# Widening the weights of an attention-and-feed-forward kernel with one shift-or instead of three bit operations

## The chip, the cores and the metric

The kernel runs on one core of one Trainium2 chip. The metric is device microseconds of one execution, from the program's start to its end as the runtime times it; a profile of one further execution gives, beside its own time, the span from its first to its last instruction. Engines are named as the profile names them: PE (TensorE matmul), PEld (its weight loads), DVE (VectorE), ACT (ScalarE), POOL (GpSimd) and SP (SyncE, which issues every DMA here).

## The reference

Attention with 4 sink keys and a window of 128 keys over 4 batches, 8 heads, 768 positions and head size 64, then a feed-forward layer over the 3072 tokens:

```python
keep = is_sink | in_window                 # first 4 keys, or 0 <= query - key < 128
a = softmax(np.where(keep, q @ k.T / 8, -1e9))
x = (a @ v) laid out as [3072, 512]
h = x @ w_in                               # [512, 2048]
g = np.where(h > 0, h, np.exp(np.minimum(h, 0)) - 1)
out = g @ w_out                            # [2048, 512]
```

The two weight matrices arrive as float64. They are 2 x 8 MB, and reach the kernel as 32 pieces of 128 rows by 512 doubles, viewed as int64.

## The kernel before, in words

**Stages.** The 24 token tiles of 128 are cut into 9 chunks of 2, 2, 2, 3, 3, 3, 3, 3, 3 tiles (`SIZES`, L42). For each chunk `attention(c)` (L503) produces x, and `feed_forward` (L756) runs over 16 steps f. A step is 12 matmuls with the w_in piece 2f into a bank h (L773), an exponential on ACT (L781), two operations that make the activation g (L783 on DVE or POOL, L784 on DVE), a float16 copy gh (L787, ACT), its float16 remainder gl (L794, POOL), and the matmuls with the w_out piece 2f+1 into banks acc (L801). Chunk 0 runs steps 0 to 6, chunk 1 steps 0 to 12, and then each its rest (`PARTS`, L45), so that chunk 0's first steps take the weight pieces as they come. Everything numeric is split into a float16 and a float16 remainder.

**The weights.** `weights(k)` (L437) makes piece k in these steps. SP loads it (L442) into one of 6 tiles raw, 128 rows of 1024 int32, that is 4 KB a row. `weight_f32` (L301) turns doubles into float32 in a tile wv: ACT reads the upper words as float32 and writes them scaled into a PSUM bank acc (L309); DVE moves 13 bits down out of the low words (L310) and the sign out of the high words (L311) into a tile wu; DVE shifts the ACT result by 3 and ORs wu into it (L312). ACT then makes the float16 part w (L463), and POOL the remainder in two halves (L464). A piece is needed by PE once its halves are there. A load waits until its raw tile is free, and until piece k - 5 has its float16 part (`AHEAD`, L50).

**The checks.** The kernel also tests that the numbers are in range: DVE reduces w (L841), the values v, which SP loads a second time into one of two tiles vm (9 loads at L845, 36 reductions at L846), and the keys and queries of chunks 4 to 8, loaded a second time likewise (20 pairs of loads at L856, 20 reductions at L860). `in_range` (L864) sums it up on DVE (L866 to L872), a matmul over the partitions follows (L882), and `decide` (L874). A branch at the very end takes `general_path` (L946) if a test fails; here it doesn't.

**What sets the order.** Every step is a task of the class `Plan` (L103) with an engine, a cost in us, its dependencies and the rings of buffers that it uses. `Plan.order` (L137) lists the tasks by assumed costs and due times, and `keep_order` (L924) fixes that order on each engine, SP's queue included: each engine runs strictly in this order, and an instruction that waits holds up all behind it. PE tasks have places of their own (`pos`), but the lines of scores, values and steps may pass each other. Where the plan leaves PE idle in the first 100 us, `with_idle_products` (L900) puts small matmuls of a constant tile hot (L886) ahead of the next step. Changed costs or dependencies thus move instructions on all engines.

Of the kernel before, what the change touches and what calls it, by code (L numbers as in the profile page):

```python
# [362 lines left out]
def fast_path(tc, ctx, first, kq, vx, wt, out, low, spread, numbers, flag):  # L363
# [68 lines left out]


    w_done = {}
    first_acc2 = []

    def weights(k):  # L437
        raw, v = raws[slot("raw")], wv[slot("wv")]

        def load():  # L440
            if wide:
                nc.sync.dma_start(raw, wt[k].bitcast(I32))  # L442
            else:
                nc.sync.dma_start(raw[:, :512].bitcast(F32), wt[k])

        def step(i):
            return lambda: weight_f32(nc, v, acc[2], wu[k % RINGS["wu"]], raw)[i]()

        ld = add("SP", 0.4, load, deps=[w_done.get(k - AHEAD, [None])[0]], lat=1.45)
        if wide:  # L450
            a = add("ACT", act_us(512), step(0), deps=[ld])
# [3 lines left out]
            ring("wu", [u1, u2], [b])  # L455
            ring("wps", [a], [b])
            ring("raw", [ld], [a, u1, u2])
            first_acc2.append(b)
# [383 lines left out]
    for c, ch in enumerate(CHUNKS):  # L842
        t, n = vm[slot("vm")], len(ch) * P
        src = vx[:, ch[0] * VT : (ch[-1] + 1) * VT].rearrange("p (g w) -> p g w", g=len(ch))
        ld = add("SP", 0.4, lambda t=t, n=n, src=src: nc.sync.dma_start(t.rearrange("p a w -> p (a w)")[:, : NP * n].rearrange("p (g w) -> p g w", w=VT), src), deps=[exps_done[NF * 4 + 8 * c]], lat=dma_us(P * NP * n * 4))  # L845
        new = [add("DVE", dve_us(n), lambda t=t, n=n, p=p, k=c * NP + p: nc.vector.tensor_reduce(v_top[:, k : k + 1], t.rearrange("p a w -> p (a w)")[:, p * n : (p + 1) * n], AX.X, ALU.max, apply_absolute_value=True), deps=[ld]) for p in range(NP)]  # L846
        ring("vm", [ld], new)
        seen += new
    for i in range((len(SIZES) - DUP) * NP):
        c, p = DUP + i // NP, i % NP  # L850
        t, n = vm[slot("vm")].rearrange("p a w -> p (a w)"), len(key_tiles(CHUNKS[c])) * KW + len(CHUNKS[c]) * P

        def both_heads(t=t, n=n, c=c, p=p):
# [92 lines left out]
def general_path(tc, ctx, kq, vx, wt, out, nw):  # L946

    nc = tc.nc
    WS = 1.0 / 256.0 if wt.dtype != F32 else 1.0
# [31 lines left out]
    wo = const.tile([P, NF, DM], F32, name="g_wo")  # L981
    for k in range(NW):
        f = k // 2
        raw = sb.tile([P, 1024], I32, name=f"g_raw{k}", tag="g_raw")
        if wt.dtype != F32:
            u = sb.tile([P, 512], I32, name=f"g_u{k}", tag="g_u")
            v = sb.tile([P, 512], F32, name=f"g_v32_{k}", tag="g_v32")
            nc.sync.dma_start(raw, wt[k].bitcast(I32))
            for step in weight_f32(nc, v, v, u, raw):
                step()  # L990
        else:
            v = raw[:, :512].bitcast(F32)
            nc.sync.dma_start(v, wt[k])
# [182 lines left out]
```

## Time and profile before

| | |
|---|---|
| time, median of 3 runs | 639.71 us (639.65 to 640.58) |
| the profiled execution's own time | 641.82 us |
| its span | 640.0 us, 13460 instructions |
| granted clock, mean | 0.987 of full speed |
| busy: PE, DVE, ACT, POOL | 615.8, 473.7, 416.6, 289.7 us |
| DMA | 95.06 MB, mean 149 GB/s |

The page gives busy times as shares of the whole span. Stages differ, so they are read below by stretches of the span. "Granted clock" is the share of TensorE's full speed that the chip allowed; 0.5 is its lower level. A busy time of PE contains matmuls at either level, and the constant products too. The DMA share is the mean share of time in which the 16 DMA engines had packets under way.

### The profile page before, as it was taken

To read this page: it belongs to the slowest core of one execution; us is meant where nothing else is said; L and a number is where in the kernel's file an instruction comes from. 1 tells how busy PE (TensorE), PEld (TensorE's weight loads), DVE (VectorE), ACT (ScalarE), POOL (GpSimd) and SP (SyncE) were. 2 spreads that over 40 slices of the span, in tenths; PEclk is the share of its full clock that TensorE was granted. 3 is DMA by queue.
4 is the path that set the end of the run, shared out by engine and by line. 5 is a ranking of instruction groups with operands and counts; after the bars stand their busy time and mean duration, and the time that the engine had idled before them with its cause. 6 is when DMAs were issued, how large, how long until landed. Compare 5 with 4: busy or idle time off the path is not lost. (4 is left out here: it accounts for less than half of the span.)

```text
span 640.0 us, 13460 instructions
## 1 busy us (share of the span) xinstructions
PE 615.8 (96%) x4537; PEld 361.2 (56%) x4537; DVE 473.7 (74%) x1248; ACT 416.6 (65%) x1192; POOL 289.7 (45%) x587
## 2 busy tenths in 40 slices
PE   7978999999999999999999999999999999999993
PEld 5645666666665555555555555555555555555551
DVE  7999899876678866687777967788777877555443
ACT  5888787877678766677667666677667666332320
POOL 4578789764334444344334445343334444222220
PEclk9978999999999999999999999999999999999997
DMA  8598858467457944475536746374425654465431
GB/s 306 154 301 224 234 220 253 135 158 185 93 127 133 198 99 107 90 210 110 117 82 158 180 96 156 82 214 106 129 74 139 162 105 100 109 189 137 115 94 61
DMA packets 120863, 95.06 MB, mean 149 GB/s; under 512 B 98132, under 2 KB 98132, under 8 KB 120788
## 3 DMA queue, kind: packets, MB, share of 16 engines
q1 hardware_dynamic: 120788, 94.14, 57.7%
q8 instruction: 37, 0.61, 0.4%
q14 instruction: 38, 0.31, 0.2%
HBM read 63.18 MB, written 7.34 MB: 110 GB/s over the span
## 5 line engine op out<-in xcount | busy, mean ns | idle before, releaser
L773 PE MATMUL h<-x,w 128*128 128x384 f16 (+1 forms) x1728 | 276.6, 310 | 3.3 <-DVE g L784 1.6
L773 PEld LDWEIGHTS <-w 128*128 128x128 f16 x1728 | 168.1, 98 | 98.1 <-POOL w L464 3.3
L794 POOL TENSOR_TENSOR gl<-g,gh 128x384 f16<-128x384 f32 (+1 forms) x144 | 125.1, 869 | 171.5 <-ACT gh L787 127.8
L801 PE MATMUL acc<-w,gh 128*128 128x512 f16 x768 | 194.2, 382 | 0.8 <-ACT gh L787 0.8
L781 ACT ACTIVATE g<-h 128x384 f32<-128x384 f32 (+1 forms) x144 | 65.3, 453 | 82.5 <-PE h L773 70.2
L787 ACT ACTIVATE gh<-g 128x384 f16<-128x384 f32 (+1 forms) x144 | 69.5, 482 | 74.4 <-DVE g L784 72.5
L801 PEld LDWEIGHTS <-gh 128*128 128x128 f16 x768 | 72.6, 98 | 74.8 <-ACT gh L787 3.7
L801 PE MATMUL acc<-w,gl 128*128 128x512 f16 x384 | 109.9, 381 | 0.2 <-POOL gl L794 0.2
L677 DVE SCALAR_TENSOR_TENSOR pq<-e,st,pq 128x256 f16<-128x256 f32 (+1 forms) x176 | 95.8, 572 | 17.3 <-ACT pq L676 16.9
L626 ACT ACTIVATE e<-e,st 128x264 f32<-128x264 f32 (+1 forms) x192 | 93.2, 486 | 14.5 <-DVE st L624 13.3
L624 DVE CUSTOM_DVE_ANT_0 e<-s,m 128x264 f32<-128x264 f32 (+1 forms) x192 | 71.5, 405 | 33.0 <-PE s L604 25.3
L784 DVE SCALAR_TENSOR_TENSOR g<-g,h 128x384 f32<-128x384 f32 (+1 forms) x144 | 72.7, 505 | 18.1 <-POOL g L783 16.7
L676 ACT ACTIVATE pq<-e,st 128x256 f16<-128x256 f32 (+1 forms) x176 | 77.2, 482 | 4.3 <-DVE st L631 3.5
L783 POOL TENSOR_SCALAR g<-g 128x384 f32<-128x384 f32 (+1 forms) x81 | 44.1, 544 | 71.0 <-ACT g L781 65.7
L801 PEld LDWEIGHTS <-gl 128*128 128x128 f16 x384 | 37.7, 98 | 46.4 <-issue 0.8
L783 DVE TENSOR_SCALAR g<-g 128x384 f32<-128x384 f32 (+1 forms) x63 | 25.1, 399 | 38.3 <-ACT g L781 38.1
L464 POOL TENSOR_TENSOR w<-wv,w 128x256 f16<-128x256 f32 x64 | 48.1, 767 | 5.6 <-ACT w L463 5.2
L532 ACT ACTIVATE kq<-kqs 128x912 f16<-128x912 f32 (+1 forms) x40 | 36.0, 913 | 17.6 <-PE s L604 15.2
L630 POOL TENSOR_SCALAR st<-st 128x2 f32<-128x2 f32 x77 | 20.0, 260 | 58.7 <-ACT e L626 55.8
L860 DVE TENSOR_REDUCE checks<-vm 128x1 f32<-128x912 f32 (+1 forms) x20 | 20.8, 1046 | 26.0 <-DMA vm<-in_kq_dram 26.0
L709 PE MATMUL po<-pt,vh 128*64 128x128 f16 x656 | 36.5, 223 | 2.3 <-DMA pt<-pq 2.3
L626 ACT ACTIVATION_READ_ACCUMULATOR e<-e,st 128x1 f32 x192 | 36.0, 188 | 0.0
(93 smaller groups left out, 658.1 us busy)
## 6 DMA issues: line engine op xcount, KB each, us to landing
raw<-in_wt_dram SPq DMA_DIRECT2D x32, 512.0 KB, 5.2
kqs<-in_kq_dram SPq DMA_DIRECT2D x24, 456.0 KB, 3.7
kqs<-in_kq_dram SPq DMA_DIRECT2D x20, 390.0 KB, 3.7
vs<-in_vx_dram SPq DMA_DIRECT2D x28, 256.0 KB, 3.3
out_dram<-wv SPq DMA_DIRECT2D x24, 256.0 KB, 2.9
vm<-in_kq_dram SPq DMA_DIRECT2D x24, 228.0 KB, 3.7
vm<-in_vx_dram SPq DMA_DIRECT2D x6, 768.0 KB, 5.1
vm<-in_kq_dram SPq DMA_DIRECT2D x16, 195.0 KB, 3.4
```

The costliest lines, as they stand in the source:

```text
L464: tls = [add("POOL", pool_us(256), lambda c=c: nc.gpsimd.tensor_tensor(w[k][:, 1, c], v[:, c], w[k][:, 0, c], ALU.subtract), deps=[th]) fo ...
L624: red = add("DVE", 0.24 + 0.001 * wd, lambda ee=ee, me=me, sp=sps[e], m=m, wd=wd, to_score=to_score: nc.vector.tensor_tensor_reduce(ee, sp ...
L626: ex = add("ACT", 0.47 + 0.00085 * wd, lambda ee=ee, me=me, rs=rs[:, e : e + 1]: nc.scalar.activation(ee, ee, AF.Exp, bias=me, scale=-1.0, ...
L676: a = add("ACT", act_us(nb * P, True), lambda src=src, hi=hi, re=re: nc.scalar.activation(hi, src, AF.Copy, scale=re), deps=[rr])
L677: b = add("DVE", 0.478 if nb == 2 else 0.33, lambda src=src, hi=hi, lo=lo, re=re: nc.vector.scalar_tensor_tensor(lo, src, re, hi, ALU.mult ...
L773: nc.tensor.matmul(hp[:, :n], win[:, part, d, :], xx[:, :n], start=k == 0, stop=k == 3 * ND - 1)
L781: a = add("ACT", act_us(n) + 0.18, lambda gf=gf, hp=hp, sums=sums: nc.scalar.activation(gf, hp[:, :n], AF.Exp, scale=1.0 / G_SCALE, accum_ ...
L783: b = add("DVE", 0.14 + 0.00057 * n, lambda gf=gf: nc.vector.tensor_scalar(gf, gf, -1.0, G_SCALE, ALU.add, ALU.mult), deps=[a], slow=2.1, ...
L784: b = add("DVE", dve_us(n), lambda gf=gf, hp=hp: nc.vector.scalar_tensor_tensor(gf, gf, 0.0, hp[:, :n], ALU.min, ALU.max), deps=[b])
L787: th = add("ACT", act_us(n), lambda gf=gf, gh=gh: nc.scalar.activation(gh[:, :n], gf, AF.Copy), deps=[b])
L794: tls.append(add("POOL", pool_us(cut), lambda gl=gl, gf=gf, gh=gh, cut=cut: nc.gpsimd.tensor_tensor(gl[:, :cut], gf[:, :cut], gh[:, :cut], ...
L801: nc.tensor.matmul(acc[i], gg[:, i * P : (i + 1) * P], wout[:, part, :], start=f == f0 and k == 0, stop=f == f1 - 1 and k == 2)
```

## The change

`weight_f32` becomes two operations. The load puts the 4096 bytes of a row 2 bytes into the tile raw (now 1025 words), so that bits 16 to 47 of each double form an aligned 32-bit word. ACT reads the top 16 bits of each double as a bfloat16 and writes it, doubled, as a float16 pattern into the upper half of each word of wu, whose lower halves were set to zero at the start by two POOL memsets. DVE shifts the aligned words of raw right by 13 and ORs the words of wu into them. L310, L311, and the PSUM bank as a stop on the way, are gone. The factor 256 of the weights is in the pattern now, in the general path 1.

The checks' loads get other dependencies: of the values chunk by chunk after exponentials 64 + 3c instead of 64 + 8c, of keys and queries after 92 + 2i instead of 94 + 2i, counted over the 144 steps in their order; and the plan assumes 2 us more for a load of keys and queries.

```diff
-def weight_f32(nc, v, d, u, raw):
-    ui = u.bitcast(U16).rearrange("p (f t) -> p f t", t=2)
-    words = raw.rearrange("p (f t) -> p f t", t=2)
-    halves = raw.bitcast(U16).rearrange("p (f t) -> p f t", t=4)
+def weight_f32(nc, v, top, raw, scale):
+    shifted = raw.bitcast(U16)
     return (
-        lambda: nc.scalar.activation(d, words[:, :, 1].bitcast(F32), AF.Copy, scale=2.0**-111),
-        lambda: nc.vector.tensor_scalar(ui[:, :, 0], halves[:, :, 1], 13, None, ALU.logical_shift_right),
-        lambda: nc.vector.tensor_scalar(ui[:, :, 1], halves[:, :, 3], 0x8000, None, ALU.bitwise_and),
-        lambda: nc.vector.scalar_tensor_tensor(v.bitcast(I32), d.bitcast(I32), 3, u, ALU.logical_shift_left, ALU.bitwise_or),
+        lambda: nc.scalar.activation(top.bitcast(F16)[:, 1::2], shifted.bitcast(BF16)[:, 4 : 4 * 512 + 1 : 4], AF.Copy, scale=scale),
+        lambda: nc.vector.scalar_tensor_tensor(v.bitcast(U32), raw.bitcast(U32)[:, 1:1025:2], 13, top.bitcast(U32), ALU.logical_shift_right, ALU.bitwise_or),
     )
+def load_weights(nc, raw, piece):
+    if piece.dtype != F32:
+        nc.sync.dma_start(raw.bitcast(U16)[:, 1:2049], piece.bitcast(U16))
...
+    for t in wu:
+        nc.gpsimd.memset(t, 0)
...
-            u1 = add("DVE", 0.446, step(1), deps=[ld], slow=2.0)
-            u2 = add("DVE", 0.446, step(2), deps=[ld], slow=2.0)
-            b = add("DVE", 0.7, step(3), deps=[a, u1, u2])
+            b = add("DVE", 0.13 + 0.00108 * 512, steps[1], deps=[a], slow=1.5)
...
-    evacs[2] = first_acc2[-1] if first_acc2 else None
...
-        ld = add("SP", 0.4, lambda t=t, n=n, src=src: ..., deps=[exps_done[NF * 4 + 8 * c]], lat=dma_us(P * NP * n * 4))
+        check_v(c, exps_done[NF * 4 + 3 * c])
-        ld = add("SP", 0.8, both_heads, deps=[exps_done[len(exps_done) - 50 + 2 * i]], lat=dma_us(P * n * 4))
+        ld = add("SP", 0.8, both_heads, deps=[after], lat=2.0 + dma_us(P * n * 4))
+        check_kq(DUP + i // NP, i % NP, len(SIZES) * NP + i, exps_done[NF * 6 - 4 + 2 * i])
```

Since the plan's costs change, the order changes on every engine. Of the constant products, 62 stand in PE's order before and 29 now. Three places follow. Line numbers of the changed kernel differ by a few: L765, L775, L776 and L793 are the old L773, L783, L784 and L801.

DVE, the last steps of chunk 8, before: L860 reduces a second load of keys and queries, L783 and L784 make the activation g, L866 is the first operation of `in_range`.

```order
L784 SCALAR_TENSOR_TENSOR g_113<-g_113,h_168 128x384
L783 TENSOR_SCALAR g_114<-g_114 128x384
L784 SCALAR_TENSOR_TENSOR g_114<-g_114,h_169 128x384
L860 TENSOR_REDUCE checks<-vm_93 128x1
L783 TENSOR_SCALAR g_113<-g_113 128x384
L784 SCALAR_TENSOR_TENSOR g_113<-g_113,h_168 128x384
L860 TENSOR_REDUCE checks<-vm_93 128x1
L783 TENSOR_SCALAR g_114<-g_114 128x384
L866 TENSOR_SCALAR checks<-checks 128x144
```

The same place with the change, up to the first operation of `in_range` (L862 now):

```order
L776 SCALAR_TENSOR_TENSOR g_114<-g_114,h_169 128x384
L775 TENSOR_SCALAR g_113<-g_113 128x384
L776 SCALAR_TENSOR_TENSOR g_113<-g_113,h_168 128x384
L775 TENSOR_SCALAR g_114<-g_114 128x384
L776 SCALAR_TENSOR_TENSOR g_114<-g_114,h_169 128x384
L775 TENSOR_SCALAR g_113<-g_113 128x384
L776 SCALAR_TENSOR_TENSOR g_113<-g_113,h_168 128x384
L775 TENSOR_SCALAR g_114<-g_114 128x384
L862 TENSOR_SCALAR checks<-checks 128x144
```

The reductions of loads no longer stand between the last steps: the last one is 24 rows ahead of L862, with eleven L776 between them.

SP's queue from its twelfth row on, before: raw are the weight loads, kqs keys and queries, vs values, pt a transpose for the values' matmuls.

```order
L524 DMA kqs_63<-in_kq_dram 128x520
L524 DMA kqs_64<-in_kq_dram 128x520
L442 DMA raw_135<-in_wt_dram 128x1024
L442 DMA raw_130<-in_wt_dram 128x1024
L524 DMA kqs_63<-in_kq_dram 128x652
L524 DMA kqs_64<-in_kq_dram 128x652
L442 DMA raw_131<-in_wt_dram 128x1024
L524 DMA kqs_63<-in_kq_dram 128x652
L546 DMA vs_65<-in_vx_dram 128x512
L695 DMA_TRANSPOSE pt_109<-pq_106 128x9x128
L524 DMA kqs_64<-in_kq_dram 128x652
L442 DMA raw_133<-in_wt_dram 128x1024
```

The same place with the change:

```order
L516 DMA kqs_63<-in_kq_dram 128x520
L516 DMA kqs_64<-in_kq_dram 128x520
L314 DMA raw_135<-in_wt_dram 128x2048
L314 DMA raw_131<-in_wt_dram 128x2048
L314 DMA raw_130<-in_wt_dram 128x2048
L516 DMA kqs_63<-in_kq_dram 128x652
L314 DMA raw_133<-in_wt_dram 128x2048
L516 DMA kqs_64<-in_kq_dram 128x652
L314 DMA raw_132<-in_wt_dram 128x2048
L516 DMA kqs_63<-in_kq_dram 128x652
L314 DMA raw_135<-in_wt_dram 128x2048
L538 DMA vs_65<-in_vx_dram 128x512
```

Of these twelve loads six are weights now, where four were.

POOL's start, before, from the memset of the constant tile ones to the end of the identity matrix:

```order
L407 MEMSET ones 128x128
L408 MEMSET hot 128x256
masks.py:197 MEMSET ident 128x128
L411 MEMSET pq_104 128x128
L411 MEMSET pq_105 128x128
L411 MEMSET pq_106 128x128
masks.py:199 AFFINE_SELECT ident<-ident 128x128
```

The same place with the change:

```order
L410 MEMSET ones 128x128
L412 MEMSET wu_128 128x512
L412 MEMSET wu_129 128x512
L413 MEMSET hot 128x256
masks.py:197 MEMSET ident 128x128
L416 MEMSET pq_104 128x128
L416 MEMSET pq_105 128x128
L416 MEMSET pq_106 128x128
masks.py:199 AFFINE_SELECT ident<-ident 128x128
```

Two memsets of 512 words each stand ahead of the rest.

## Rows read from the trace of the kernel before

**Rows 1.** The span in five stretches: us, busy (x instructions) by engine, clock, DMA.

```profile
0.00:28.00 28.00, 23.32 (x169) 16.19 (x170) 23.18 (x97) 19.06 (x60) 13.47 (x43) 1.00 0.71 240
28.00:70.00 42.00, 34.07 (x291) 21.51 (x289) 38.45 (x98) 34.21 (x99) 33.62 (x64) 0.88 0.93 253
70.00:120.00 50.00, 49.08 (x379) 32.10 (x377) 44.83 (x106) 41.27 (x116) 39.72 (x71) 1.00 0.72 223
120.00:600.00 480.00, 479.11 (x3559) 276.96 (x3558) 351.86 (x915) 314.87 (x902) 196.21 (x403) 1.00 0.56 132
600.00:640.00 40.00, 30.17 (x149) 14.47 (x147) 15.38 (x34) 7.19 (x20) 6.72 (x9) 0.92 0.27 77
```

**Rows 2.** The same columns, PE, PEld and POOL alone: constant products, 28 to 70 us.

```profile
28.00:70.00 42.00, 4.17 (x37) 3.11 (x35) 0.00 (x0) 0.88 0.93 253
```

**Rows 3.** Who PE waited for, 28 to 70 us: total, times, longest.

```profile
PE s L609 <- DVE st L624: 4.3, 2, 3.7
PE h L773 <- DVE g L784: 1.6, 1, 1.6
PE h L773 <- POOL w L464: 1.1, 1, 1.1
```

**Rows 4.** Timeline of PE, 42 to 75 us: start, us, operation, count.

```profile
42.51 2.74 PE L773 MATMUL h<-x,w 128*128 128x256 f16 x12
...
56.35 2.33 PE L773 MATMUL h<-x,w 128*128 128x256 f16 x11 [1.11 <-POOL w L464]
...
73.53 1.47 PE L773 MATMUL h<-x,w 128*128 128x256 f16 x12
```

**Rows 5.** Groups of instructions by line and shape: busy us, mean ns, idle before.

```profile
L312 DVE SCALAR_TENSOR_TENSOR wv<-acc,wu 128x512 int32<-128x512 int32 x32 | 21.8, 681 | 1.3 <-ACT acc L309 1.2
...
L310 DVE TENSOR_SCALAR wu<-raw 128x512 uint16<-128x512 uint16 x32 | 20.3, 634 | 0.2 <-DMA raw<-in_wt_dram 0.2
...
L309 ACT ACTIVATE acc<-raw 128x512 f32<-128x512 f32 x32 | 20.1, 629 | 1.8 <-DVE wv L312 1.6
...
L463 ACT ACTIVATE w<-wv 128x512 f16<-128x512 f32 x32 | 19.8, 619 | 0.3 <-DVE wv L312 0.3
...
L558 DVE SCALAR_TENSOR_TENSOR vl<-vs,vh 128x512 f16<-128x512 f32 x23 | 18.2, 799 | 0.8 <-ACT vh L557 0.7
...
L846 DVE TENSOR_REDUCE checks<-vm 128x1 f32<-128x384 f32 x24 | 12.2, 537 | 0.0
```

**Rows 6.** DVE busy with L310, L311 and L312 alone, by stretch.

```profile
0.00:28.00 28.00, 7.48 (x14) 1.00 0.71 240
28.00:70.00 42.00, 17.46 (x28) 0.88 0.93 253
```

**Rows 7.** Timeline of POOL and DVE at the start.

```profile
1.55 0.30 POOL L408 MEMSET hot<- 128x256 bf16 x1
...
2.39 0.28 POOL masks.py:199 TENSOR_SCALAR_AFFINE_SELECT ident<-ident 128x128 f32<-128x128 f32 x1
```

**Rows 8.** The same, DVE's first instruction.

```profile
1.23 1.53 DVE L331 CAST pt<-pt 128x128 f32<-128x128 int32 x1 [1.23 <-POOL pt L328]
```

**Rows 9.** Timeline of PE, a score matmul of chunk 0's third pair of heads.

```profile
14.75 0.49 PE L609 MATMUL s<-kqs 64*128 64x132 f32 x4 [0.20 <-DMA kqs<-in_kq_dram]
```

**Rows 10.** Timeline of the last steps, ACT, DVE and PE.

```profile
623.04 0.19 ACT L781 ACTIVATION_READ_ACCUMULATOR g<-h 128x1 f32 x1
...
625.47 0.81 PE L801 MATMUL acc<-w,gl 128*128 128x512 f16 x3
625.58 1.10 DVE L860 TENSOR_REDUCE checks<-vm 128x1 f32<-128x912 f32 x1 [3.37 <-DMA vm<-in_kq_dram]
...
626.60 0.35 DVE L783 TENSOR_SCALAR g<-g 128x384 f32<-128x384 f32 x1
...
629.33 0.61 PE L801 MATMUL acc<-w,gh 128*128 128x512 f16 x2 [0.84 <-ACT gh L787]
```

**Rows 11.** DMA issues, 28 to 70 us: count, KB each, median us to landing.

```profile
raw<-in_wt_dram SPq DMA_DIRECT2D x11, 512.0 KB, 4.8
```

More of the change, by code (lines that the diff above doesn't have):

```diff
@@ L14 @@
 U16 = mybir.dt.uint16
+U32 = mybir.dt.uint32
 AF = mybir.ActivationFunctionType
@@ L296, in dma_us @@
     return nbytes / 330e3
-def weight_f32(nc, v, d, u, raw):
-    ui = u.bitcast(U16).rearrange("p (f t) -> p f t", t=2)
-    words = raw.rearrange("p (f t) -> p f t", t=2)
-    halves = raw.bitcast(U16).rearrange("p (f t) -> p f t", t=4)
+def weight_f32(nc, v, top, raw, scale):
+    shifted = raw.bitcast(U16)
     return (
-        lambda: nc.scalar.activation(d, words[:, :, 1].bitcast(F32), AF.Copy, scale=2.0**-111),
-        lambda: nc.vector.tensor_scalar(ui[:, :, 0], halves[:, :, 1], 13, None, ALU.logical_shift_right),
-        lambda: nc.vector.tensor_scalar(ui[:, :, 1], halves[:, :, 3], 0x8000, None, ALU.bitwise_and),
-        lambda: nc.vector.scalar_tensor_tensor(v.bitcast(I32), d.bitcast(I32), 3, u, ALU.logical_shift_left, ALU.bitwise_or),
-    )
+        lambda: nc.scalar.activation(top.bitcast(F16)[:, 1::2], shifted.bitcast(BF16)[:, 4 : 4 * 512 + 1 : 4], AF.Copy, scale=scale),
+        lambda: nc.vector.scalar_tensor_tensor(v.bitcast(U32), raw.bitcast(U32)[:, 1:1025:2], 13, top.bitcast(U32), ALU.logical_shift_right, ALU.bitwise_or),
+    )
+def load_weights(nc, raw, piece):
+    if piece.dtype != F32:
+        nc.sync.dma_start(raw.bitcast(U16)[:, 1:2049], piece.bitcast(U16))
+    else:
+        nc.sync.dma_start(raw[:, :512].bitcast(F32), piece)
 def elu(nc, g, h, scale):
@@ L393, in fast_path @@
     wu = rows("wu", [P, 512], I32)
-    raws = rows("raw", [P, 1024], I32)
+    raws = rows("raw", [P, 1025], I32)
     w = rows("w", [P, 2, 512], F16, NW)
@@ L434, in fast_path @@
     w_done = {}
-    first_acc2 = []
     def weights(k):
         raw, v = raws[slot("raw")], wv[slot("wv")]
[L440 to L449, printed above, removed]
-        if wide:
-            a = add("ACT", act_us(512), step(0), deps=[ld])
-            u1 = add("DVE", 0.446, step(1), deps=[ld], slow=2.0)
-            u2 = add("DVE", 0.446, step(2), deps=[ld], slow=2.0)
-            b = add("DVE", 0.7, step(3), deps=[a, u1, u2])
[L455 to L458, printed above, removed]
+        top = wu[k % RINGS["wu"]]
+        ld = add("SP", 0.4, lambda: load_weights(nc, raw, wt[k]), deps=[w_done.get(k - AHEAD, [None])[0]], lat=1.45)
+        if wide:
+            steps = weight_f32(nc, v, top, raw, 2.0)
+            a = add("ACT", act_us(512), steps[0], deps=[ld])
+            b = add("DVE", 0.13 + 0.00108 * 512, steps[1], deps=[a], slow=1.5)
+            ring("wu", [a], [b])
+            ring("raw", [ld], [a, b])
         else:
@@ L841, in fast_path, with check_v, check_kq, both_heads @@
     seen = [add("DVE", 0.5, lambda k=k: nc.vector.tensor_reduce(w_top[:, k : k + 1], w[k][:, 0, :], AX.X, ALU.max, apply_absolute_value=True), deps=[w_done[k][0], exps_done[NF * 4 + 2 * k]]) for k in range(NW)]
[L842 to L846, printed above, removed]
-        ring("vm", [ld], new)
[L848 to L853, printed above, removed]
+    def check_v(c, after):
+        t, n = vm[slot("vm")].rearrange("p a w -> p (a w)"), SIZES[c] * P
+        src = vx[:, CHUNKS[c][0] * VT : (CHUNKS[c][-1] + 1) * VT].rearrange("p (g w) -> p g w", g=SIZES[c])
+        ld = add("SP", 0.4, lambda: nc.sync.dma_start(t[:, : NP * n].rearrange("p (g w) -> p g w", w=VT), src), deps=[after], lat=dma_us(P * NP * n * 4))
+        new = [add("DVE", dve_us(n), lambda p=p, k=c * NP + p: nc.vector.tensor_reduce(v_top[:, k : k + 1], t[:, p * n : (p + 1) * n], AX.X, ALU.max, apply_absolute_value=True), deps=[ld]) for p in range(NP)]
+        ring("vm", [ld], new)
+        seen.extend(new)
+    def check_kq(c, p, k, after):
+        t, n = vm[slot("vm")].rearrange("p a w -> p (a w)"), len(key_tiles(CHUNKS[c])) * KW + SIZES[c] * P
+        def both_heads():
             for e in range(2):
@@ L856, in both_heads @@
                 nc.sync.dma_start(t[r, :n], kq[r, o : o + n])
-        k = len(SIZES) * NP + i
-        ld = add("SP", 0.8, both_heads, deps=[exps_done[len(exps_done) - 50 + 2 * i]], lat=dma_us(P * n * 4))
-        new = [add("DVE", dve_us(n), lambda t=t, n=n, k=k: nc.vector.tensor_reduce(v_top[:, k : k + 1], t[:, :n], AX.X, ALU.max, apply_absolute_value=True), deps=[ld])]
+        ld = add("SP", 0.8, both_heads, deps=[after], lat=2.0 + dma_us(P * n * 4))
+        new = [add("DVE", dve_us(n), lambda: nc.vector.tensor_reduce(v_top[:, k : k + 1], t[:, :n], AX.X, ALU.max, apply_absolute_value=True), deps=[ld])]
         ring("vm", [ld], new)
-        seen += new
+        seen.extend(new)
+    for c in range(len(SIZES)):
+        check_v(c, exps_done[NF * 4 + 3 * c])
+    for i in range((len(SIZES) - DUP) * NP):
+        check_kq(DUP + i // NP, i % NP, len(SIZES) * NP + i, exps_done[NF * 6 - 4 + 2 * i])
     def in_range():
@@ L948, in general_path @@
     nc = tc.nc
-    WS = 1.0 / 256.0 if wt.dtype != F32 else 1.0
+    WS = 1.0
     const = ctx.enter_context(tc.tile_pool(name="g_const", bufs=1))
@@ L983, in general_path @@
         f = k // 2
-        raw = sb.tile([P, 1024], I32, name=f"g_raw{k}", tag="g_raw")
+        raw = sb.tile([P, 1025], I32, name=f"g_raw{k}", tag="g_raw")
+        load_weights(nc, raw, wt[k])
         if wt.dtype != F32:
@@ L987, in general_path @@
             v = sb.tile([P, 512], F32, name=f"g_v32_{k}", tag="g_v32")
-            nc.sync.dma_start(raw, wt[k].bitcast(I32))
-            for step in weight_f32(nc, v, v, u, raw):
+            nc.gpsimd.memset(u, 0)
+            for step in weight_f32(nc, v, u, raw, 1.0):
                 step()
@@ L992, in general_path @@
             v = raw[:, :512].bitcast(F32)
-            nc.sync.dma_start(v, wt[k])
         dst = wo[:, f, :] if k % 2 else wi[:, :, f * P : (f + 1) * P]
```

## The prediction, made before the changed kernel was run

> **What bounds the kernel now.** The first view to read is the table of stretches, because the page's shares hide where PE is idle. From 120 to 600 us PE is busy 479.11 of 480 us [rows 1]: nothing is to be had there, and whatever other engines save there costs or gives nothing. From 70 to 120 us it idles 0.9 us. The three places with room are the first 28 us (4.7 us idle), 28 to 70 us (7.9 us idle, and the only long stretch where the clock falls, to 0.88), and the last 40 us (9.8 us idle). So the question is what the change does in the first 70 us and in the last 20.
>
> In 28 to 70 us chunk 0's first seven steps take the weight pieces as they come, beside chunk 1's attention. DVE is busy 38.45 of 42 us, ACT 34.21, POOL 33.62, and the DMA share is 0.93 [rows 1]. DVE is the fullest, and the waits of PE agree: 4.3 us for L624, 1.6 us for L784, both on DVE, 1.1 us for POOL's half of a weight piece [rows 3]. There is more loss than those waits. After each of the two long stalls PE runs at the lower level, 1.2 GHz: twelve L773 take 2.74 us where 1.47 is normal at full speed, eleven 2.33 where 1.47 x 11/12 = 1.35 would be [rows 4]. These two groups alone lose 1.27 + 0.98 = 2.25 us. And 4.17 us go to constant products [rows 2], which are no work.
>
> At the end, the order of DVE sets it. The last step's exponential and its sum are done at 623.23, but L783 starts at 626.60, because a reduction of a second load (L860) stands ahead of it and waited 3.37 us for its DMA. PE has finished everything else at 626.28 and starts the last step's L801 at 629.33 [rows 10].
>
> **The change part by part.** The profiled execution spans 640.0 us and took 641.82 us itself; the median is 639.71. I sum against the span, and carry the difference to the median.
>
> *Price of a piece on DVE.* Removed: L310 at 634 ns, and L311, the same operation on other halves. L312 at 681 ns becomes one shift-or of the same 512 columns, both inputs in SBUF now. It is not in the trace. Its nearest row is L558, same width and both inputs in SBUF: 799 ns against 681 for L312, which reads PSUM [rows 5]. Bounds 0.68 to 0.80; I take 0.80, the row with the same kinds of inputs. A piece saves 1.27 - 0.12 = 1.15 us of DVE. On ACT a 512-column copy into PSUM (629 ns, L309) becomes one into SBUF (619 ns, L463) [rows 5]: nothing.
>
> *The start.* Two memsets of 512 words are new on POOL, ahead of the rest of its constants. L408 takes 0.30 us for 256 columns [rows 7], so 0.5 to 0.6 us each, about 1.05 together. Who waits? DVE's first cast takes 1.53 us for 128 columns and ends at 2.76, right after POOL's run of small operations ends at 2.39 + 0.28 = 2.67 [rows 7, 8]; it seems to be held until POOL pauses. All masks and the first scores come behind it. Cost between 0 and +1.05; I take **+1.0**.
>
> *0 to 28 us.* The three operations take 7.48 us of DVE [rows 6], of which four L312 are 2.7; so 4.8 go, and 0.5 come back: 4.3 us less of 23.18. DVE is not last everywhere: the third pair's scores wait for their keys at 14.75 [rows 9], and relief before that is lost. Bounds 0 and -4.3; roughly half the stretch lies behind that wait: **-2**.
>
> *28 to 70 us.* 17.46 us [rows 6], less ten L312 (6.8), are 10.65 us removed; 1.2 come back: 9.5 us less. DVE then has 29.0 us of work, and something else is last. If it is ACT, whose 34.21 us nothing shortens, the stretch can give 7.8 us; if the DMA engines' 0.93 is all work, 2.9; if the wait only changes its name, nothing. I take **-6**: PE's two waits for DVE are 5.9 us [rows 3], and the 2.25 us of lower clock and part of the 4.17 us of constant products (33 of 62 are gone from the order) are room for the new wait. The earlier weight loads in SP's queue help; a late transpose ahead of them holds them up as before.
>
> *The middle.* The value checks come in 24 steps of 144, where they came in 64. Six more loads' reductions fall there, 24 x 0.537 = 12.9 us [rows 5] on about 107 us (24/144 of the span, an estimate). DVE goes from 351.86/480 = 73% [rows 1] to some 85%, less than the 90% of 70 to 120 us beside a gapless PE. Cost 0 to 1 us; I take 0, PE's stock of ready steps hides it.
>
> *The end.* No reduction of a load stands in DVE's last 24 rows before the tests. L783 can start at 623.23 instead of 626.60. From its start to L801 it was 629.33 - 626.60 = 2.73 us, with the tests between; so L801 would be ready at 625.96, and PE is free at 626.28, plus 0.16 for the matmul of the tests. L801 at 626.45: **-2.9**. Below that lies nothing but a late DMA again (0).
>
> Sum: +1.0 - 2 - 6 - 2.9 = -9.9. That is 630.1 us of span, and **629.8 us** for the median.
>
> *A rule against the change.* Before, each weight row lands at the tile's start; now 2 bytes on, and no row of before shows such a landing. The Trainium skill ("Collectives: The Full Stack", Rules for kernel authors) asks for buffers at 32-byte multiples, since otherwise the hardware reads, modifies and writes; that speaks against the shifted load, and no run here shows it yet. The Trainium skill ("DMA: Bandwidth & Descriptors", How a descriptor splits into AXI transactions) counts only one more transaction for a 4096-byte row that starts off a 256-byte boundary, 129 beats for 128, an estimate of under 1%, and by that the sum stays as it is.
>
> **The rivals.**
>
> A. *Another engine is last at once.* ACT, the DMA engines or SP's queue take over in the first 70 us. For it: ACT is at 81%, DMA at 0.93 [rows 1]. Against it: at 70 to 120 us PE runs without gaps beside ACT at 83% and DVE at 90%. Then only start and end count: 639.7 + 1.0 - 2.9 = 637.8 us.
>
> B. *The full relief.* The first stretch gives its 4.3, the second the 7.8 that ACT allows: 639.7 + 1.0 - 4.3 - 7.8 - 2.9 = 625.7 us. Against it: strict orders rarely let an engine run full.
>
> C. *Slower: the shifted load.* If a row landing 2 bytes on costs the DMA engines more, weights come late. At 253 GB/s [rows 1] a 512 KB load takes 2.07 us of all engines; 11 are issued in 28 to 70 us [rows 11], 22.8 us, and the stretch has 0.07 x 42 = 2.9 us to spare. At twice the cost it grows by 19.9 us: 639.7 + 1.0 + 19.9 - 2.9 = 657.7. The gain elsewhere is -1.9 with start and end alone, so this rival decides from 4.8 us more in 11 loads, that is 21% more for each. For it stands no row, only that the landing is new; against it, the rows stay 4096 bytes long, and their number stays.
>
> D. *The change doesn't do what it says:* the shift-or takes 1.95 us, as the three did. Then the early terms vanish, and it is case A.
>
> **How the numbers follow.** My forecast (near 630, its own range 626 to 634) has 0.58. A with D has 0.22, B 0.10, C 0.07, and 0.03 are for no difference. 0.2% (1.3 us, about what a measurement here can tell from none) puts the border of "faster" at 638.4. A at 637.8 lies just inside, so I count a fifth of it as the same. Faster: 0.58 + 0.10 + 0.17 = 0.85; same 0.05 + 0.03 = 0.08; slower 0.07. The range must reach to A and B, since forecast alone leaves more than 2 in 10 out: 624.5 to 638.0, which also takes in the bounds of the start and of the stretch to 70 us.
>
> **What would show it.** Right: L310 and L311 gone and the shift-or at 0.7 to 0.8 us; DVE in 28 to 70 us well below 38; PE without gaps from about 61 us on; no dip of the clock at 40 and 57 us; L801's last group within 0.2 us of the group before it. The cast at the start ends near 3.8 us. Wrong: weight loads that land in over 6 us in that stretch (C); PE idle and clock as before with ACT, POOL or a DMA named as its releaser (A); a DVE that again waits for a DMA in the last ten steps (the end's term).

## The result and the profile after

The changed kernel takes 631.99 us (median of 4 runs, 631.36 to 632.39), the kernel before on the same chip 639.68 us (639.19 to 640.58, 4 runs). The ratio is 0.9868, with a 95% interval of 0.9851 to 0.9885. The forecast was 629.8 us in a range of 624.5 to 638.0. The profiled execution took 632.12 us, and its span is 9.7 us shorter than before. That is more than the 7.7 us between the medians, because the profiled execution of the kernel before took 641.82 us, 2.1 us above its median; differences between the two traces hold this too.

The page of the changed kernel, its span and part 1, and below it the five stretches, with the columns of [rows 1]:

```profile
span 630.3 us, 13327 instructions
PE 608.5 (97%) x4504; PEld 357.1 (57%) x4504; DVE 451.4 (72%) x1187; ACT 418.8 (66%) x1192; POOL 291.2 (46%) x586
```

```profile
0.00:28.00 28.00, 20.38 (x141) 13.90 (x143) 21.50 (x81) 18.80 (x53) 18.30 (x49) 1.00 0.77 263
28.00:70.00 42.00, 36.13 (x315) 22.73 (x316) 31.05 (x96) 34.97 (x103) 30.26 (x68) 0.96 0.90 242
70.00:120.00 50.00, 48.95 (x375) 31.62 (x373) 39.05 (x85) 42.52 (x114) 40.05 (x68) 1.00 0.79 230
120.00:600.00 480.00, 479.69 (x3559) 277.19 (x3558) 351.80 (x903) 316.30 (x909) 197.42 (x399) 1.00 0.56 136
600.00:630.30 30.30, 23.30 (x123) 11.68 (x121) 8.03 (x25) 6.23 (x17) 5.23 (x6) 0.93 0.08 29
```

To compare them, PE's constant products must come off its busy time. The same view of their line alone (PE, PEld, clock, DMA), before in the first and third stretch, and after in the first two (it has none later):

```profile
0.00:28.00 28.00, 4.46 (x27) 2.88 (x27) 1.00 0.71 240
...
70.00:120.00 50.00, 0.34 (x4) 0.07 (x1) 1.00 0.72 223
```

```profile
0.00:28.00 28.00, 4.82 (x25) 2.88 (x25) 1.00 0.77 263
28.00:70.00 42.00, 0.58 (x4) 0.31 (x4) 0.96 0.90 242
```

Idle time and constant products together are the time in which PE has no work of the task: 28 - 23.32 + 4.46 = 9.14 us before [rows 1], 12.44 us after. So the first 28 us got **worse by 3.3 us**. From 28 to 70 us it falls from 12.10 us [rows 1, 2] to 6.45 us (-5.65), from 70 to 120 from 1.26 to 1.05, from 120 to 600 from 0.89 to 0.31. These make -3.1 us. The last matmul of L765 ends at 617.35 us where that of L773 ended at 622.39: -5.0. The rest, -1.9 us, is task work that runs in less time; the only stretch before 600 us whose clock changed is 28 to 70 us (0.88 to 0.96), so I put it there (the first experiment below shows that it need not come from the weights). From that last matmul to the end of the span it was 17.61 us and is 12.95: **-4.65 us**.

The start and the first step of the feed-forward part: POOL's clears, DVE's first cast, the longest wait of PE for a diagonal (L630 is the old L638), and PE's first step.

```profile
1.55 0.98 POOL L412 MEMSET wu<- 128x512 int32 x2
...
1.23 2.45 DVE L334 CAST pt<-pt 128x128 f32<-128x128 int32 x1 [1.23 <-POOL pt L331]
...
17.76 3.01 POOL L457 TENSOR_TENSOR w<-wv,w 128x256 f16<-128x256 f32 x4
...
21.13 0.67 POOL L457 TENSOR_TENSOR w<-wv,w 128x256 f16<-128x256 f32 x1
21.75 1.06 POOL L630 TENSOR_TENSOR pq<-ident,st 128x256 f32<-128x256 f32 x1
...
22.87 0.71 PE L636 MATMUL acc<-pq,e 128*128 128x128 f32 x4 [1.33 <-POOL pq L630]
...
32.46 2.79 PE L765 MATMUL h<-x,w 128*128 128x256 f16 x24
```

```profile
28.07 1.47 PE L773 MATMUL h<-x,w 128*128 128x256 f16 x12
```

The cast ends at 3.68 instead of 2.76 us [rows 8]. Since weights are ready earlier, POOL has 12 of their halves (L457, 8.78 us) between 10 and 30 us instead of 6 (3.97 us), and its diagonals stand behind them. The diagonals take longer too, eight of them, before and after:

```profile
L638 POOL TENSOR_TENSOR pq<-ident,st 128x256 f32<-128x256 f32 x8 | 5.2, 647 | 7.3 <-DVE st L631 7.3
```

```profile
L630 POOL TENSOR_TENSOR pq<-ident,st 128x256 f32<-128x256 f32 x8 | 6.6, 826 | 3.5 <-DVE st L623 3.1 <-PE acc L636 0.4
```

The first step starts at 32.46 us, 4.4 us later than before (the two rows of L765 and L773 above), though two steps then run back to back.

The prices, groups by line: busy us, mean ns, idle before.

```profile
L308 DVE SCALAR_TENSOR_TENSOR wv<-raw,wu 128x512 uint32<-128x512 uint32 x32 | 29.2, 920 | 4.0 <-ACT wu L307 2.4 <-POOL w L457 1.4
L307 ACT ACTIVATE wu<-raw 128x512 f16<-128x512 bf16 x32 | 24.1, 771 | 2.7 <-DMA raw<-in_wt_dram 2.7
```

The shift-or takes 920 ns, not 800, and ACT's copy 771 ns where L309 took 629 [rows 5]. In 28 to 70 us the waits, of PE and then of ACT, are now:

```profile
PE po L701 <- DVE x L740: 1.9, 1, 1.9
PE h L765 <- DVE g L776: 1.5, 2, 1.1
PE po L701 <- DMA pt<-pq: 1.1, 1, 1.1
...
PE s L601 <- DVE st L616: 0.5, 1, 0.5
```

```profile
ACT wu L307 <- DMA raw<-in_wt_dram: 2.7, 2, 2.4
ACT vh L549 <- DMA vs<-in_vx_dram: 2.3, 1, 2.3
```

PE's 4.3 us for DVE's L624 [rows 3] are 0.5 us now (L616). ACT waits 5.0 us for loads, where it was 2.6 before. One dip of the clock is left: the stretch 49 to 56 us has 0.76, and in it twelve L765 take 2.67 us.

```profile
52.32 2.67 PE L765 MATMUL h<-x,w 128*128 128x256 f16 x12 [0.36 <-DVE g L776]
```

The end of the changed kernel, timeline of DVE and PE, and of the kernel before its last matmul; below each the stretch of the last matmuls (columns as in [rows 1]):

```profile
619.65 0.55 DVE L776 SCALAR_TENSOR_TENSOR g<-g,h 128x384 f32<-128x384 f32 x1
...
620.43 0.81 PE L793 MATMUL acc<-w,gl 128*128 128x512 f16 x3
...
621.10 0.59 PE L793 MATMUL acc<-w,gh 128*128 128x512 f16 x2
...
622.92 0.38 PE L793 MATMUL acc<-w,gl 128*128 128x512 f16 x1
```

```profile
621.00:624.00 3.00, 2.30 (x12) 0.73 (x9) 2.16 (x7) 0.60 (x1) 0.56 (x1) 1.00 0.13 48
```

```profile
632.66 0.63 PE L801 MATMUL acc<-w,gl 128*128 128x512 f16 x1
```

```profile
629.00:634.00 5.00, 3.77 (x9) 1.00 (x9) 2.23 (x7) 0.87 (x2) 0.67 (x1) 0.66 0.25 91
```

No reduction of a load stands before the last step now, and L793's last group starts as the group before it ends. Moreover the last nine matmuls take 2.20 us (621.10 to 623.30) where they took 3.96 (629.33 to 633.29) [rows 10]: before, PE had stood still for about 3 us just ahead of them and got a clock of 0.66, now it is 1.00. Of the 1.76 us between the two, 0.19 are a wait for POOL's remainder gl among the nine, so 1.57 us go with the clock.

### The profile page after: what moved, and what is told of

The parts are those of the page before. It is cut to its first block, busy times and chain, and to the rows that moved or that the text cites. A ratio compares the mean times of both kernels' runs of the same rounds, so it can differ in the third digit from the quotient of the medians.

```text
span 630.3 us, 13327 instructions
## 1 busy us (share of the span) xinstructions
PE 608.5 (97%) x4504; PEld 357.1 (57%) x4504; DVE 451.4 (72%) x1187; ACT 418.8 (66%) x1192; POOL 291.2 (46%) x586
## 4 chain that ended last, share of the span: by engine, by line
PE 90%; POOL 4%; DVE 2%; issue 2%; DMA 1%; ACT 0%; POOLq 0%; DVEq 0%; ACTq 0%
PE acc L793 39%; PE h L765 38%; PE po L701 5%; PE s L601 3%; PE s L595 2%; PE s L596 2%; POOL w L457 2%; DMA pt<-pq 1%; PE h L882 1%; DMA vs<-in_vx_dram 1%; POOL pq L630 1%; PE po L706 1%; DVE pt L334 0%; PE acc L636 0%; DVE wv L308 0%
## 5 line engine op out<-in xcount | busy, mean ns | idle before, releaser
L765 PE MATMUL h<-x,w 128*128 128x384 f16 (+1 forms) x1728 | 275.0, 309 | 1.5 <-DVE g L776 1.5
L765 PEld LDWEIGHTS <-w 128*128 128x128 f16 x1728 | 167.8, 98 | 94.9 <-issue 3.4
L793 PE MATMUL acc<-w,gh 128*128 128x512 f16 x768 | 192.8, 379 | 1.0 <-POOL w L457 1.0
L773 ACT ACTIVATE g<-h 128x384 f32<-128x384 f32 (+1 forms) x144 | 65.2, 453 | 102.2 <-PE h L765 93.0
L793 PEld LDWEIGHTS <-gh 128*128 128x128 f16 x768 | 72.4, 98 | 70.8 <-ACT g L773 1.4
L793 PE MATMUL acc<-w,gl 128*128 128x512 f16 x384 | 109.2, 379 | 0.0
L616 DVE CUSTOM_DVE_ANT_0 e<-s,m 128x264 f32<-128x264 f32 (+1 forms) x192 | 71.8, 405 | 32.8 <-PE s L596 21.5
L776 DVE SCALAR_TENSOR_TENSOR g<-g,h 128x384 f32<-128x384 f32 (+1 forms) x144 | 72.9, 506 | 14.2 <-POOL g L775 12.4
L775 POOL TENSOR_SCALAR g<-g 128x384 f32<-128x384 f32 (+1 forms) x79 | 43.2, 547 | 79.1 <-ACT g L773 75.8
L775 DVE TENSOR_SCALAR g<-g 128x384 f32<-128x384 f32 (+1 forms) x65 | 27.1, 417 | 69.0 <-ACT g L773 68.9
L793 PEld LDWEIGHTS <-gl 128*128 128x128 f16 x384 | 37.5, 98 | 46.7 <-POOL gl L786 0.9
L457 POOL TENSOR_TENSOR w<-wv,w 128x256 f16<-128x256 f32 x64 | 48.9, 786 | 6.1 <-ACT w L456 5.5
L701 PEld LDWEIGHTS <-vh 128*64 128x64 f16 x656 | 26.6, 109 | 14.6 <-issue 14.0
```

Source lines behind the costliest of these rows:

```text
L616: red = add("DVE", 0.24 + 0.001 * wd, lambda ee=ee, me=me, sp=sps[e], m=m, wd=wd, to_score=to_score: nc.vector.tensor_tensor_reduce(ee, sp ...
L701: nc.tensor.matmul(po[e * D : (e + 1) * D, oc], vts[i][x][:, vo : vo + D], pt[:, (2 * e + part) * nb + i, :], start=new, stop=last)
L765: nc.tensor.matmul(hp[:, :n], win[:, part, d, :], xx[:, :n], start=k == 0, stop=k == 3 * ND - 1)
L773: a = add("ACT", act_us(n) + 0.18, lambda gf=gf, hp=hp, sums=sums: nc.scalar.activation(gf, hp[:, :n], AF.Exp, scale=1.0 / G_SCALE, accum_ ...
L775: b = add("DVE", 0.14 + 0.00057 * n, lambda gf=gf: nc.vector.tensor_scalar(gf, gf, -1.0, G_SCALE, ALU.add, ALU.mult), deps=[a], slow=2.1, ...
L776: b = add("DVE", dve_us(n), lambda gf=gf, hp=hp: nc.vector.scalar_tensor_tensor(gf, gf, 0.0, hp[:, :n], ALU.min, ALU.max), deps=[b])
```

## The experiments

**The two halves of the change apart.** First the new weights with the checks' old dependencies and the plan's old cost of their loads:

```diff
-        ld = add("SP", 0.8, both_heads, deps=[after], lat=2.0 + dma_us(P * n * 4))
+        ld = add("SP", 0.8, both_heads, deps=[after], lat=dma_us(P * n * 4))
-        check_v(c, exps_done[NF * 4 + 3 * c])
+        check_v(c, exps_done[NF * 4 + 8 * c])
-    check_kq(..., exps_done[NF * 6 - 4 + 2 * i])
+    check_kq(..., exps_done[len(exps_done) - 50 + 2 * i])
```

> The changed kernel with the checks' loads at their old places and old assumed latency. Theory 1 (two separate parts: the weights give the first 120 us, the checks the end): the end loses its 3 us again, about 635 us, and PE's last group of L793 waits for a gh as L801 did before; the first 120 us read as in the changed kernel. Rival 2 (the checks' places give nothing, since the whole order was drawn anew and the end fell right by chance): within 1 us of the changed kernel, 632. Rival 3 (the order as a whole is worth more than its parts): the start changes too and the time is anywhere between 632 and 640.

Then the old weights with the checks of the change (the same lines the other way round, in the kernel before):

> The kernel before with the new places and latency of the checks' loads alone, weights as before. Theory 1: only the end gains, 3 us, about 636.7 us; L310 and L311 are as before and so are the stalls near 37 and 54 us. Rival 2: no difference from before, 639.7. Rival 4 (the gain is nearly all in the checks, and the weights only moved waits): 633 us or less.

Measured, beside 640.25 us for the kernel before: the weights alone 637.06 us, ratio 0.994 (0.992 to 0.996); the checks alone 638.0 us, 0.9962 (0.9949 to 0.9975). So the parts give 3.2 and 2.3 us where both together give 7.7, and the 635 and 636.7 us of the theories were missed by 2.1 and 1.3 us. Whether the parts truly give less singly stays open, since the intervals of the ratios still allow a plain sum. In the traces the parts stand at different places. With the weights alone the last L765 ends at 617.23 us, as with both, and 18.8 us follow; with the checks alone the last L773 ends at 623.12 and 13.2 us follow. Against the trace before, the weights are worth -5.2 us up to the last step, the checks -4.4 us behind it. In the run with the weights alone DVE again waits in its last 37 us for loads of keys and queries, and the last matmuls again run at a clock of 0.66:

```profile
DVE checks L851 <- DMA vm<-in_kq_dram: 13.3, 5, 3.6
```

```profile
624.00:629.00 5.00, 3.77 (x9) 1.01 (x9) 2.15 (x7) 0.94 (x2) 0.67 (x1) 0.66 0.23 85
```

The run with the checks alone is the better partner for the early stretches: it has the old weights, its profiled execution (638.05 us) is at its median, and its clock in 28 to 70 us is 0.96, as in the changed kernel. That stretch (columns as in [rows 1]), and below it the constant products alone:

```profile
28.00:70.00 42.00, 31.52 (x277) 19.87 (x277) 38.56 (x98) 34.07 (x97) 33.46 (x64) 0.96 0.95 246
```

```profile
28.00:70.00 42.00, 3.78 (x32) 2.70 (x30) 0.96 0.95 246
```

PE is without task work for 14.26 us there, and for 6.45 us with the new weights too: -7.8 us, with no change of clock. Over all stretches this time falls by 5.75 us from the one run to the other, and the last matmul into h (L773, now L765) ends 5.77 us earlier (623.12 to 617.35). So the gain of the weights up to there is accounted for by less waiting alone; the 1.9 us by the clock in the trace before are not shown to be a gain of their own.

**The constant products.** Both kernels without any (`IDLE_UNTIL = 0.0`), since 33 of them went with the change:

> The kernel before without its 62 constant products. They took 9.0 us of PE before and 5.4 us in the changed kernel, and this difference is half of what PE has less to do. Theory 6 (they only fill time in which PE would wait anyway, and hold the clock): the time stays or grows by 0 to 4 us by a lower clock before 70 us. Rival 7 (they stand in the way, so that the 33 fewer of them are a real gain of the change): the time falls by 2 to 5 us.

> The changed kernel without any constant product. Theory (they only fill time in which PE would stand still, and hold the clock): 631.5 to 634 us, like the kernel before, which lost 0.3% without them; PE's busy time in 28 to 120 us falls by their 5.4 us and its idle time rises by about as much. Rival (the 33 products that went with the change were work on the path, and so a part of the gain): without the rest it is faster by some of the 5.4 us that are left, 627 to 630 us.

Measured: the kernel before 641.91 us, 1.0026 (1.001 to 1.0042); the changed one 631.5 us, 0.986 (0.9836 to 0.9883), no different from 0.9868. The products are no load that the change took off the path. In the changed kernel, without them, the other matmuls of the first 28 us grow instead. The diagonals' matmuls, with products and without:

```profile
L636 PE MATMUL acc<-pq,e 128*128 128x128 f32 x40 | 6.5, 297 | 2.1 <-POOL pq L630 2.1
```

```profile
L636 PE MATMUL acc<-pq,e 128*128 128x128 f32 x36 | 8.5, 396 | 0.4 <-POOL pq L630 0.3
```

**The start.** The clears of the word tiles on ACT (idle there) instead of POOL, behind the memset of hot, which ACT reads:

```diff
-        nc.gpsimd.memset(t, 0)
+        nc.scalar.activation(t.bitcast(F32)..., hot..., AF.Copy, scale=0.0)
```

> The changed kernel with the tiles wu set to zero by two ACT copies instead of two POOL memsets. Theory 1 with the cast held by POOL's run of small operations: DVE's first cast ends at 2.8 instead of 3.7 us, everything in the first 28 us comes 0.9 us earlier, and the time falls by 0.9 us, to 631.1. Rival 5 (the first stretch is set by the arrival of keys behind five weight loads, so the start is hidden): the cast ends earlier, the first L765 does not, and the time stays at 632.0.

Measured: 631.03 us, 0.9852 (0.9832 to 0.9872). The cast takes 1.53 us again, the first step starts at 31.71 instead of 32.46 and the last L765 ends 1.4 us earlier, at 615.99. The intervals overlap those of the changed kernel, so the trace shows the place and the time only suggests it.

**POOL's halves ahead of the diagonals.** The plan may put the halves on DVE as well (31 of 64 go there), and the same with the clears on ACT:

```diff
-... deps=[th])
+... deps=[th], or_=("DVE", 0.41, lambda c=c: nc.vector.tensor_tensor(...)))
```

> The changed kernel, but the order may put a weight piece's remainder halves on VectorE too (0.41 us in the plan), where before it had no room for them; nothing else. Theory (the first step of the feed-forward part starts at 32.5 us instead of 28.1 because POOL now takes 13 halves between 10 and 30 us, ahead of the diagonals that PE waits for): PE's 2.1 us of waits for the diagonals nearly go, the first step starts at or before 30.5 us, and the time is 629 to 631 us. Rival (the delay comes from VectorE and ScalarE, the shift-or at 0.9 and the copy at 0.77 us): the first step starts at 32 us or later, and the time is 632 to 635 us.

> The same, with the two clears of the word tiles on ScalarE instead of POOL. If both pieces are independent: the 1 us of the clears comes off the run with the halves alone, 628 to 630 us. If what is won at the start is lost again before 70 us: no more than the better of the two alone, 630.5 to 631.5 us.

Measured: 631.88 us, 0.9876 (0.9858 to 0.9894), and 631.85 us, 0.987 (0.9853 to 0.9887). In the first the waits for diagonals fall from 2.1 to 0.9 us and the first step starts at 31.36 us; in the second at 30.86. So the halves and, less surely, the clears are in the delay, with 1.1 and 0.5 to 0.8 us of its 4.4, and neither time moves. (These are single traces; in the run with unshifted rows below, whose order is that of the changed kernel, the first step starts at 32.03 us instead of 32.46.) What is won by 28 us (12.44 to 11.48 us without task work in the first) is lost by 70 (6.45 to 7.87), where the next waits are, PE's and ACT's:

```profile
PE po L701 <- DVE x L740: 3.3, 2, 2.7
...
ACT wu L307 <- DMA raw<-in_wt_dram: 3.2, 2, 1.7
```

Neither theory was met by the first: the step starts later than the one said and earlier than the other, and the time lies between their ranges. The second lies above both of its ranges. An earlier first step did not shorten these two runs.

**The prices by themselves.** A prelude of repeated operations, ahead of the changed kernel:

```diff
+        for _ in range(3):
+            nc.scalar.activation(f[:, 1::2], sh[:, 4 : 4 * 512 + 1 : 4], AF.Copy, scale=2.0)
+        for _ in range(3):
+            nc.scalar.activation(f[:, :512], sh[:, 4 : 4 * 512 + 1 : 4], AF.Copy, scale=2.0)
...
```

> The changed kernel with a prelude that measures prices: on ScalarE, three times each, 512 columns as 16-bit float with every second 16-bit place written, from bfloat16 8 bytes apart (as the change does); the same written without gaps; with gaps from bfloat16 without gaps; neither with gaps; from 32-bit float 8 bytes apart with gaps; and 32 bits to 32 bits from 8 bytes apart. Then four shift-ors on VectorE with POOL idle, then six beside POOL's remainder halves. The whole is some 20 us longer for it. Theory for ScalarE (the extra 0.14 us is the gap in the write): 0.77 where the write has gaps, 0.62 where not. Rival (the 16-bit read with gaps): 0.77 in the first two, 0.62 in the others. Theory for VectorE (it shares a way into SBUF with POOL): 0.68 alone and 0.9 to 1.2 beside POOL, whose halves then take over 0.67. Rival (the price is its own): 0.9 in both.

Measured (649.24 us in one run, with the prelude), groups by line on ACT: the six forms in the order of the text above are L424, L426, L428, L430, L432 and L434. Below them the timeline of the shift-ors (L436 and L440) and of POOL's halves:

```profile
L432 ACT ACTIVATE wu<-raw 128x512 f16<-128x512 f32 x3 | 2.3, 775 | 0.1
L428 ACT ACTIVATE wu<-raw 128x512 f16<-128x512 bf16 x3 | 2.3, 764 | 0.0
L424 ACT ACTIVATE wu<-raw 128x512 f16<-128x512 bf16 x3 | 2.3, 761 | 0.0
L426 ACT ACTIVATE wu<-raw 128x512 f16<-128x512 bf16 x3 | 2.0, 660 | 0.1
...
L434 ACT ACTIVATE wv<-raw 128x512 f32<-128x512 f32 x3 | 1.9, 645 | 0.0
...
L430 ACT ACTIVATE wu<-raw 128x512 f16<-128x512 bf16 x3 | 1.9, 629 | 0.1
```

```profile
20.10 0.68 DVE L436 SCALAR_TENSOR_TENSOR wv<-raw,wu 128x512 uint32<-128x512 uint32 x1
20.70 2.84 DVE L440 SCALAR_TENSOR_TENSOR wv<-raw,wu 128x512 uint32<-128x512 uint32 x3
...
20.87 6.32 POOL L438 TENSOR_TENSOR w<-wv,w 128x256 f16<-128x256 f32 x8 [10.02 <-DVE wv L436]
```

ACT's extra 0.14 us is the gap in the written 16-bit places: 761 to 775 ns with it, 629 to 660 without, however the input lies. The shift-or takes 0.68 to 0.69 us seven times with POOL idle. Of the three that overlap POOL's halves, the first, begun 0.17 us ahead of POOL, still takes 0.69 us, and the other two take 1.04 us each. POOL's first three halves take 1.04 to 1.11 us, and the five behind the last shift-or 0.66 each. So either engine is held up while the other works, and the one that came first is not slowed. The Trainium skill ("SBUF — State Buffer", two separate sides) describes the port pair that the two engines share as an exclusive lock, held for the whole instruction by whichever starts first of a VectorE operation with two SBUF inputs and a GpSimd operation that reads SBUF. These numbers agree.

**The shift of the load.** Rows at the tile's start again (the lower weight bits then come from the wrong place):

```diff
-        nc.sync.dma_start(raw.bitcast(U16)[:, 1:2049], piece.bitcast(U16))
+        nc.sync.dma_start(raw.bitcast(U16)[:, 0:2048], piece.bitcast(U16))
```

> The changed kernel, but each row of words lands at the tile's start again, as before the change; the copy reads its 16 bits one place further on and the shift-or the even 32-bit words, so the lower bits of the weights are taken from the wrong place and nothing else differs. Theory (the 2 bytes of shift cost the transfers nothing): landing of the weight loads within 0.5 us of the 4.6 us median, and the same time as the changed kernel within 0.2%, 631 to 633 us. Rival (the shift costs, and hid in the order): landing under 4.1 us, and 627 to 630 us.

Measured: 632.08 us, 0.9867 (0.9847 to 0.9887), as with the shift. Landing of the 32 loads (count, KB, median us to landing): shifted, unshifted, and the kernel before.

```profile
raw<-in_wt_dram SPq DMA_DIRECT2D x32, 512.0 KB, 4.6
```

```profile
raw<-in_wt_dram SPq DMA_DIRECT2D x32, 512.0 KB, 4.7
```

```profile
raw<-in_wt_dram SPq DMA_DIRECT2D x32, 512.0 KB, 5.2
```

**Who is last in 28 to 70 us now.** ACT waits there for loads that stand in SP's queue behind the transposes (L687), which wait 8.4 us for DVE:

```profile
SPq L687 <- DVE pq L669: 8.4, 3, 4.5
```

The value loads go to ACT's queue, or the weight loads behind the sixth do:

```diff
-                ld = add("SP", 0.4, lambda: nc.sync.dma_start(st, vx[...]), ...)
+                ld = add("ACT", 0.1, lambda: nc.scalar.dma_start(st, vx[...]), ...)
```

> The changed kernel, but the value loads (L538) are issued by ScalarE's own queue instead of standing behind the transposes of the probabilities in SP's. Theory (what is last in 28 to 70 us after the change are loads that stand in SP's queue behind transposes, which wait 8.4 us for VectorE there): ScalarE's 2.3 us of wait for a value load go, PE's busy time in that stretch rises by over 1 us, and the time is 628 to 630.5 us. Rival (the DMA engines are full there, share 0.90): the waits only change their name, 631 to 633 us.

> The changed kernel, but the weight loads after the sixth are issued by ScalarE's own queue. Theory (loads stand behind transposes in SP's queue): ScalarE's 2.7 us of waits for words in 28 to 70 us go, and the time is 628 to 630.5 us. Rival (the DMA engines are full there): the waits stay, 631 to 633 us. It would be slower, 633 to 636 us, if ScalarE, at 83% of that stretch, is held up by a load that waits for its buffer.

Measured: the value loads 629.16 us, 0.9839 (0.9819 to 0.9859), which still touches the interval of the changed kernel; the weight loads 645.47 us, 1.0075 (1.005 to 1.0099), above all three of the expected ranges. With the value loads moved the 2.3 us for them are gone and the clock is 1.00 in the stretch:

```profile
28.00:70.00 42.00, 37.46 (x348) 24.76 (x347) 30.52 (x91) 35.96 (x106) 29.97 (x66) 1.00 0.92 234
```

```profile
ACT wu L307 <- DMA raw<-in_wt_dram: 2.9, 3, 2.5
```

PE's busy time rises by 1.33 us, but that is constant products (5.18 us instead of 0.58); what the stretches show as gained is the dip of the clock and the 1.05 us of idle time from 70 to 120 us. The first step starts at 31.42 us, 1.0 us earlier, so the place of the value loads in SP's queue is another candidate for its delay. So the time and ACT's wait went as the theory had it, PE's work did not, and how much of it is the queue and how much the new order stays open. With the weight loads moved, the transposes in SP's queue wait 21.4 us in total for DVE in that stretch. That the weights came too late, because ACT reaches the place of their loads in its order late, was only argued.

**The best of both.** Clears on ACT and value loads on ACT's queue:

> The changed kernel with the two edits that came out lowest: the word tiles cleared by ScalarE (alone 631.0 us) and the value loads issued by ScalarE's queue (alone 629.2 us). If the 0.9 us of the start reach the end, 627.5 to 629 us, with the first step of the feed-forward part near 30.7 us and the step at 66.6 us at 65.5 or earlier. If the stretch to 70 us swallows them, as it did with the remainder halves, 629 to 630.5 us.

Measured: 628.69 us (628.5 to 629.45), 0.983 (0.9817 to 0.9844), below both kernels. The first step starts at 31.54 us, and the later step that starts at 66.56 us with the value loads alone starts at 66.57, so the theory's two marks (30.7 and 65.5) failed; the interval doesn't tell it from the value loads alone.

## Why the prediction was right, point by point

The sum came near: -9.9 us were forecast, the spans differ by 9.7 us and the medians, without the slow profiled execution of before, by 7.7. In part that is luck. By the spans the first 28 us came out 4.3 us worse than forecast, and the other terms (28 to 70 us by 1.5, the middle by 0.8, the end by 1.8) better by 4.1, so that the errors cancel.

- **Start, +1.0**: right. The two clears take 0.98 us, the cast ends 0.92 us later.
- **0 to 28 us, -2**: wrong in sign. With the start the stretch was to give -1.0 us and costs 3.3. DVE is relieved (busy 23.18 to 21.50), but the step asked only what DVE loses in work. It did not ask what earlier weights do to POOL, whose busy time goes from 13.47 to 18.30 us and whose diagonals PE waits for. The runs show two pieces of the 4.4 us at the first step, the halves (1.1 us) and the clears (up to 0.8). Two more are candidates: the diagonals themselves, 826 ns instead of 647 (1.4 us over eight; that they are held up by the shift-or, as the halves are, was not tested), and the value loads in SP's queue (1.0). With clears and value loads moved together the step starts no earlier than with the value loads alone (31.54, 31.42), so the pieces don't add up; how the delay divides stays open.
- **28 to 70 us, -6**: right in place and mechanism, low in size: -5.65 us without task work and about -1.9 by the clock against the trace before, -7.8 without task work against the checks alone. DVE's 31.05 us are near the forecast 29.0, and PE's long wait for it is gone. Two of the signs held only in part: one of the two dips of the clock is left, and PE is not without gaps from 61 us on (it still waits 1.1 us for a transpose at 63 to 64 us).
- **The constant products as "room"**: wrong. Without them neither kernel gets faster.
- **Middle, 0**: -0.8 us; the added reductions cost nothing that shows.
- **End, -2.9**: right in mechanism, too small. The wait gave 3.2 us (6.94 us from the last step's L773 to the last group before, 3.75 after); left out was the clock, 1.57 us in the last nine matmuls.
- **Prices**: the shift-or at 0.80 was the row with the right inputs, but what decides is POOL beside it: 0.69 alone, 0.92 in the kernel. ACT's "nothing" was +0.14 us a piece; the rows compared had no gaps in what they write.
- **Rivals**: A (637.8) is start and end alone; the weights' -5 us up to the last step decide against it. What it names seems to come next: ACT's waits for loads in SP's queue (5.0 us in 28 to 70 us). B (625.7) fell on the first stretch. C fell: landing 4.6 us against 5.2 before and 4.7 unshifted. The alignment rule of the Trainium skill ("Collectives: The Full Stack", Rules for kernel authors) gives a read-modify-write as its reason and no price; no run here shows a cost of the shift (631.99 and 632.08 us). D fell with 0.92 against 1.95 us.

## What to carry to other kernels

When an engine is relieved, ask which other engine gets its work earlier, and what stands behind that work in strict order: here POOL got weight halves ahead of the diagonals that PE needs. Cost a wait ahead of PE with the matmuls behind it too, since they may run at the lower clock. Where idle time is filled by a plan, compare time without task work, not idle time. Before a difference between two traces is shared out, look how far each profiled execution lies from its median: here about 2 of 9.7 us were that.

## What was not expected of the hardware

- Without constant products eight L636 take 2.08 us early in the changed kernel (from 13.30 us) where they take 1.16 with them (from 13.13), while the granted clock reads 1.00 in both. That column doesn't show everything that slows a matmul.
- ACT pays 0.10 to 0.14 us per 512 columns for writing every second 16-bit place, and under 0.04 us for reading with gaps (one run, each form three times).
- Two bytes of shift in 4096-byte rows cost nothing that 32 loads or the time show.
